# Twelve x tiles turned by VectorE from square blocks instead of by TensorE, in a fused attention and token-mixer kernel

## The chip, the cores and the metric

The kernel runs on one core of one Trainium2 chip. The metric is the device time of one execution in microseconds. A core has TensorE (PE, with its weight loads shown apart as PEld), VectorE (DVE), ScalarE (ACT), GpSimd (POOL) and SyncE (SP), which here issues nearly all DMAs. The engines run their own instruction streams and meet at semaphores.

## What is computed

x is 2048 tokens by 512 channels. Two branches read it, and a gate per token mixes them. All arrays are float32.

```python
def _A_ref(x, wqkv, wo):                       # B=1, S=2048, D=512, 32 heads of 16
    qkv = (x @ wqkv).reshape(B, S, 3, H, Dh).transpose(2, 0, 3, 1, 4)
    q, k, v = qkv[0], qkv[1], qkv[2]
    p = softmax(einsum("bhqd,bhkd->bhqk", q, k) * Dh ** -0.5, axis=-1)
    o = einsum("bhqk,bhkd->bhqd", p, v)
    return o.transpose(0, 2, 1, 3).reshape(B, S, D) @ wo

def _B_ref(x, w1, b1, w2, b2):                 # token mixer, F=1792
    h = layernorm(x, axis=-1)
    u = gelu(einsum("bsd,sf->bdf", h, w1) + b1)
    y = einsum("bdf,fs->bds", u, w2) + b2
    return y.transpose(0, 2, 1)

g = sigmoid((x * gate_w).sum(-1, keepdims=True))
return g * a + (1 - g) * b
```

## The kernel before

To keep float32 accuracy, every operand of a large matmul is split into a high part (a cast to float32r, by ACT) and a low part (the difference, by DVE or POOL); a product is three matmuls: high by high, high by low, low by high (`split` and `products`, L80 to L91).

The program runs through stages in this order, by the times of the profile: the V stage (to about 58 us), the projection of q and k (to 145 us), the mixer's first layer (to 297 us), and then attention with the mixer's second layer mixed in, until the end. PE works without a pause nearly all the way, so a stage begins when PE is done with the one ahead.

The V stage is what the change touches. It works on x in 16 tiles of 128 tokens. For each tile it does three things:

- The tile is turned, since a matmul contracts over partitions and x has its channels along the free axis. `turn(t)` has PE transpose the tile's four 128x128 chunks into a PSUM bank (L201); `turned(t)` casts the result into `xt_hi` (ACT) and subtracts into `xt_lo` (DVE, reading PSUM and SBUF). These two hold all of turned x, for V and later for q and k.
- V of the tile is computed: twelve matmuls (`products` with `v_pairs`, L90), then a copy out of PSUM by ACT (`v_out`, L235).
- `row_stats(t)` has DVE take the mean and the variance of each row (L212, L213) and the product with the gate's weights, summed (L215). These are needed later, for the layer norm and the gate.

The first two tiles are mixed with the arrival of the V weights in an order written out by hand (`tc.manual_schedule`, from L237). From tile 2 on a loop turns tile t + 1, takes the statistics of tile t - 2 and computes V of tile t; there the framework orders each engine's instructions by its own planner, except where `keep_in_program_order` holds them. SP loads each x tile with one DMA (`load`, L186) into one of six buffers. A DMA into a buffer waits until the last reader of the buffer is done, and whatever SP issues later stands behind it.

The weights of q and k come by `wcols` (L172), 128 columns at a time, in chunks k of 128 rows: chunk k of the turned x holds channels 128k to 128k + 127. Two of them are fetched and split within the loop, at t = 8 and t = 12. The biases of the mixer are loaded as rows, and PE turns them (L227) at t = 4.

Of the kernel before, what the change touches and what calls it, by code (L numbers as in the profile page):

```python
# [10 lines left out]
F32 = mybir.dt.float32  # L11
# [4 lines left out]
ALU = mybir.AluOpType  # L16
# [6 lines left out]
P = 128  # L23
S = 2048
D = 512
F = 1792
H = 32
DH = 16
NS = S // P
ND = D // P  # L30
NF = F // P
NB = 512
NQ = S // NB
VC = DH + 1
SCALE = DH**-0.5
# [40 lines left out]
def gated_mix(ctx: ExitStack, tc: tile.TileContext, a_x, a_wqkv, a_wo, b_w1, b_b1, b_w2, b_b2, gate_w, out):  # L76
    nc = tc.nc
    xf, of = (t.rearrange("b s d -> (b s) d") for t in (a_x, out))

    def split(hi, lo, src, copy, sub):  # L80

        copy(hi, src)  # L82
        return sub(lo, src, hi.bitcast(F32), ALU.subtract)  # L83

    def products(ps, pairs, start=True, stop=True):

        n, last = 0, 3 * len(pairs) - 1
        for (lh, ll), (rh, rl) in pairs:
            for a, b in ((lh, rh), (lh, rl), (ll, rh)):
                nc.tensor.matmul(ps, a, b, start=start and n == 0, stop=stop and n == last)  # L90
                n += 1  # L91
# [7 lines left out]
    ident = const.tile([P, P], F32, name="ident")  # L99
    make_identity(nc, ident)  # L100
    b1 = const.tile([P, NF], F32, name="b1")
    b2x2 = const.tile([P, NS], F32, name="b2x2")
    z = const.tile([P, NS], F32, name="z")
# [9 lines left out]
    v = v_pool.tile([P, NS, H, VC], F32, name="v")  # L113
# [5 lines left out]
    def bank():  # L119
        return acc.tile([P, NB], F32, name="acc")  # L120


    xt_pool = xt_ctx.enter_context(tc.tile_pool(name="xt", bufs=1, side="right"))
    xt_hi = xt_pool.tile([P, ND, S], F32R, name="xt_hi")
    xt_lo = xt_pool.tile([P, ND, S], F32R, name="xt_lo")
# [9 lines left out]
    loaded, ready, subs = [], [], []  # L135
# [27 lines left out]

    qk = qk_ctx.enter_context(tc.tile_pool(name="qk", bufs=2, side="right"))

    def wcols(c0):
        raw = qk.tile([P, ND, P], F32, name="wc_raw")
        hi = qk.tile([P, ND, P], F32R, name="wc_hi", bufs=3)
        lo = qk.tile([P, ND, P], F32R, name="wc_lo", bufs=3)
        src = a_wqkv[:, c0 : c0 + P].rearrange("(k p) c -> p k c", p=P)  # L170
        with tc.issue_after(x_load.ins):
            nc.sync.dma_start(raw, src)  # L172
        split(hi, lo, raw, nc.scalar.copy, nc.gpsimd.tensor_tensor)
        return hi, lo

    qk_cols = [c0 + b * P for b in range(ND) for c0 in (D, 0)]
    qk_w = []
    x_load = None

    with tc.tile_pool(name="vp", bufs=1, side="right") as pool:  # L180
        xs = {}

        def load(t):
            nonlocal x_load
            xs[t] = pool.tile([P, D], F32, name="x", bufs=6)
            x_load = nc.sync.dma_start(xs[t], xf[t * P : (t + 1) * P, :])  # L186

        gw = pool.tile([P, D], F32, name="gw")
        wv = []

        def load_wv(k):
            raw = pool.tile([P, D], F32, name=f"wv_raw{k}")
            nc.sync.dma_start(raw, a_wqkv[k * P : (k + 1) * P, 2 * D : 3 * D])  # L193
            wv.append((raw, pool.tile([P, D], F32R, name=f"wv_hi{k}"), pool.tile([P, D], F32R, name=f"wv_lo{k}")))

        turns = {}

        def turn(t, later=False):
            turns[t] = acc.tile([P, ND, P], F32, name="acc")
            for k in range(ND):  # L200
                nc.tensor.transpose(turns[t][:, k, :], xs[t][:, k * P : (k + 1) * P], ident)  # L201
            if not later:
                turned(t)

        def turned(t):
            cols = slice(t * P, (t + 1) * P)
            split(xt_hi[:, :, cols], xt_lo[:, :, cols], turns[t], nc.scalar.copy, nc.vector.tensor_tensor)

        def row_stats(t):

            st = pool.tile([P, 6], F32, name="stats", bufs=3)
            tc.keep_in_program_order(nc.vector.bn_stats(st, xs[t]))  # L212
            nc.vector.bn_aggr(mv[:, t, :], st)  # L213
            junk = pool.tile([P, D], F32, name="junk")
            dot = nc.vector.scalar_tensor_tensor(  # L215
                junk, xs[t], 1.0, gw, ALU.mult, ALU.mult, accum_out=z[:, t : t + 1]
            )
            tc.keep_in_program_order(dot)

        def biases(pool):  # L220
            for n, (src, dst, rows, mul) in enumerate(((b_b1, b1, NF, 1.0), (b_b2, b2x2, NS, 2.0))):

                t = pool.tile([P, P], F32, name=f"bias{n}")
                nc.gpsimd.memset(t, 0.0)
                nc.sync.dma_start(t[:rows], src.rearrange("(r c) -> r c", c=P))
                pt = bank()[:, :P]
                nc.tensor.transpose(pt, t, ident)  # L227
                nc.vector.tensor_scalar_mul(dst, pt[:, :rows], mul)

        def v_pairs(t):  # L230
            cols = slice(t * P, (t + 1) * P)
            return [((xt_hi[:, k, cols], xt_lo[:, k, cols]), wv[k][1:]) for k in range(ND)]

        def v_out(t, ps):
            nc.scalar.copy(v[:, t, :, 0:DH], ps.rearrange("p (h d) -> p h d", d=DH))  # L235

        with tc.manual_schedule():  # L237

            idle = pool.tile([P, NB], BF16, name="idle")
            nc.vector.memset(idle, 0.0)  # L240
            warm_ps = bank()

            def warm(n):
                for _ in range(n):
                    nc.tensor.matmul(warm_ps, idle[:, :P], idle, start=True, stop=True)

            warm(6)
            load(0)
            load_wv(0)
            load_wv(1)  # L250
            load(1)
            load_wv(2)
            load_wv(3)
            for t in (2, 3):
                load(t)
            nc.sync.dma_start(gw, gate_w[None, :].broadcast_to([P, D]))

            def split_wv(k):
                raw, hi, lo = wv[k]
                split(hi, lo, raw, nc.scalar.copy, nc.vector.tensor_tensor)  # L260


            two_ps = [bank(), bank()]

            def part(k, *which, last=False):

                for n, (t, a, b) in enumerate(which):
                    nc.tensor.matmul(  # L268
                        two_ps[t],
                        (xt_hi, xt_lo)[a][:, k, t * P : (t + 1) * P],  # L270
                        wv[k][1 + b],
                        start=k == 0 and a == b == 0,
                        stop=last and n >= len(which) - 2,
                    )

            split_wv(0)
            turn(0)
            warm(2)
            part(0, (0, 0, 0), (0, 0, 1), (0, 1, 0))
            split_wv(1)  # L280
            turn(1, later=True)
            part(1, (0, 0, 0), (0, 1, 0), (0, 0, 1))
            turned(1)
            part(0, (1, 0, 0), (1, 0, 1))
            part(1, (1, 0, 0), (1, 0, 1))
            part(0, (1, 1, 0))
            part(1, (1, 1, 0))
            both = [(t, *ab) for ab in ((0, 0), (1, 0), (0, 1)) for t in range(2)]
            split_wv(2)
            part(2, *both)  # L290
            split_wv(3)
            turn(2)
            part(3, *both, last=True)
            for t in range(2):
                v_out(t, two_ps[t])
        nc.gpsimd.memset(v[:, :, :, DH:VC], 1.0)
        load(4)
        load(5)
        for t in range(2, NS):
            if t + 4 < NS:  # L300
                load(t + 4)
            if t + 1 < NS:
                turn(t + 1)
            if t == 4:
                biases(pool)
            if t in (8, 12):
                qk_w.append(wcols(qk_cols.pop(0)))
            row_stats(t - 2)
            ps = bank()
            products(ps, v_pairs(t))  # L310
            v_out(t, ps)
        for t in range(NS - 2, NS):
            row_stats(t)
        pool.tile([P, 40], F32, name="pad")
        e = pool.tile([P, NS], F32, name="e")
        nc.scalar.activation(e, z, AF.Exp, scale=-1.0)
        nc.vector.tensor_scalar_add(e, e, 1.0)
        nc.vector.reciprocal(g, e)
        nc.vector.tensor_scalar(omg, g, -0.5, 0.5, ALU.mult, ALU.add)
        y, t, w = (pool.tile([P, NS], F32, name=n) for n in "ytw")  # L320
        nc.vector.tensor_scalar_add(w, mv[:, :, 1], EPS)
        nc.scalar.activation(y, w, AF.Sqrt)
        nc.vector.reciprocal(y, y)

        nc.vector.tensor_mul(t, y, y)
        nc.vector.tensor_mul(t, t, w)
        nc.vector.tensor_scalar(t, t, -0.5, 1.5, ALU.mult, ALU.add)
        nc.vector.tensor_mul(rs, y, t)
# [270 lines left out]
    rows = {}  # L599
# [581 lines left out]
```

## Time and profile before

| | |
|---|---|
| time, median of 3 runs | 1277.91 us |
| lowest and highest run | 1277.29, 1278.1 us |
| span of the profiled execution | 1276.0 us (its own time is not given apart; the span lies 1.9 us under the median) |
| PE busy | 1266.6 us (99%) |
| ACT, DVE, POOL busy | 1071.9 (84%), 719.3 (56%), 210.8 us (17%) |
| V stage's loop, tile 2's matmuls to the start of tile 14's | 13.66 to 52.33 us |

Rows of groups read: line, engine, operation, output<-inputs, shapes, count | busy us, mean ns of one | idle time of the engine before them and what ended it. Rows of the timeline read: start us, duration us, engine, line, operation, output<-inputs, and in brackets the idle time before. Rows of the chain read: start us, duration us, engine and line. Rows of windows give the busy time of each engine in a stretch, with the count of instructions, then the granted TensorE clock, the share of the 16 DMA engines in use, and GB/s. Rows of waits read: waiting engine and line, what it waited for, us in total, times, longest.

### The profile page before, as it was taken

The page shows a single profiled execution, that of the slowest core. Times are in us where ns is not written, and L with a number is a line of the kernel's source. Part 1 is how long each engine was busy: PE and PEld are TensorE (multiplying, and loading weights), DVE is VectorE, ACT ScalarE, POOL GpSimd, SP SyncE. Part 2 cuts the span into 40 slices and gives each one's busy share as a digit, 9 for nine tenths or more (in the row PEclk, how much of TensorE's full clock was granted, in tenths as well). Part 3 has the DMA queues.
Part 4 walks back from the last instruction along what each step waited for, and adds up shares of the span by engine and source line. Part 5 has one row for each costly group of instructions (what it writes and reads, how often), then busy time and mean ns, then how long its engine had stood idle before and what let it go on. Part 6 is the DMA issues. An engine that isn't in the chain of part 4 may idle for free.

```text
span 1276.0 us, 33051 instructions
## 1 busy us (share of the span) xinstructions
PE 1266.6 (99%) x13278; PEld 801.2 (63%) x13278; DVE 719.3 (56%) x1329; ACT 1071.9 (84%) x1484; POOL 210.8 (17%) x435
## 2 busy tenths in 40 slices
PE   9999999999999999999999999999999999999998
PEld 7888888886555555555555555555555555555555
DVE  5675363528776766666634346676666662325425
ACT  3444343437999999999999999999999999999994
POOL 0210144454111111111110011111111111100000
PEclk9999999999999999999999999999999999999999
DMA  4497743328443333433555533333343345446721
GB/s 133 141 304 274 241 122 99 99 71 166 84 93 59 74 76 70 79 70 76 116 107 115 129 77 69 69 72 76 68 78 72 74 82 109 98 88 198 149 62 70
DMA packets 94641, 137.37 MB, mean 108 GB/s; under 512 B 16313, under 2 KB 55375, under 8 KB 91408
## 3 DMA queue, kind: packets, MB, share of 16 engines
q1 hardware_dynamic: 93904, 134.14, 44.8%
q8 instruction: 106, 1.74, 0.6%
q10 hardware_dynamic: 576, 1.05, 0.2%
q14 instruction: 55, 0.45, 0.1%
HBM read 99.10 MB, written 36.03 MB: 106 GB/s over the span
## 4 chain that ended last, share of the span: by engine, by line
PE 99%; DMA 0%; ACT 0%; SPq 0%; DVE 0%; issue 0%
PE s L826 37%; PE s L868 34%; PE acc L429 12%; PE acc L90 10%; PE dn L989 4%; PE pa L1060 1%; PE acc L201 1%; PE dn L857 0%; PE acc L268 0%; DMA x<-in_A_x_dram 0%; ACT pt L891 0%; PE pa L1069 0%; SPq L193 0%; DVE base L1082 0%; SPq L186 0%
## 5 line engine op out<-in xcount | busy, mean ns | idle before, releaser
L891 ACT ACTIVATE pt<-s 128x512 f32<-128x512 f32 (+1 forms) x1259 | 943.5, 962 | 10.0 <-PE s L868 4.3
L868 PE MATMUL s<-qs,ks 64*128 64x512 f32 x2048 | 493.9, 404 | 0.8 <-POOL token L993 0.5
L826 PE MATMUL s<-pt,v 128*17 128x256 f32 x8024 | 482.6, 381 | 0.0
L868 PEld LDWEIGHTS s<-qs,ks 64*128 64x128 f32 x2048 | 325.4, 184 | 168.7 <-ACT pt L891 91.0
L846 DVE TENSOR_TENSOR ot<-s,ot 128x256 f32<-128x256 f32 (+2 forms) x427 | 190.4, 447 | 348.9 <-PE s L826 271.6
L826 PEld LDWEIGHTS s<-pt,v 128*17 128x17 f32 x8024 | 210.4, 97 | 232.2 <-ACT pt L891 84.2
L989 PE MATMUL dn<-u_hi,w_hi 64*128 64x512 f32 x428 | 186.4, 436 | 0.0
L83 POOL TENSOR_TENSOR w_lo<-w_raw,w_hi 128x512 fp32r<-128x512 f32 (+1 forms) x126 | 149.7, 1189 | 167.3 <-ACT w_hi L82 107.3
L989 PE MATMUL dn<-u_lo,w_hi 64*128 64x512 f32 x430 | 169.8, 395 | 0.0
L989 PE MATMUL dn<-u_hi,w_lo 64*128 64x512 f32 x430 | 169.2, 394 | 0.0
L993 POOL MEMSET token<- 1x1 f32 x256 | 26.2, 102 | 779.4 <-PE dn L989 711.8
L913 DVE SCALAR_TENSOR_TENSOR row<-row,o_hi 128x512 f32<-128x512 f32 x168 | 116.6, 694 | 4.9
L82 ACT CAST w_hi<-w_raw 128x512 fp32r<-128x512 f32 (+1 forms) x67 | 38.1, 569 | 79.4 <-PE acc L429 58.9
L429 PE MATMUL acc<-h_hi,w_hi 128*128 128x512 f32 x224 | 87.1, 389 | 0.0
L429 PE MATMUL acc<-h_lo,w_hi 128*128 128x512 f32 x224 | 87.1, 389 | 0.0
L429 PE MATMUL acc<-h_hi,w_lo 128*128 128x512 f32 x224 | 87.1, 389 | 0.0
L989 PEld LDWEIGHTS dn<-u_hi,w_lo 64*128 64x128 f32 x430 | 79.3, 184 | 1.3
L989 PEld LDWEIGHTS dn<-u_lo,w_hi 64*128 64x128 f32 x430 | 79.4, 185 | 0.4
L989 PEld LDWEIGHTS dn<-u_hi,w_hi 64*128 64x128 f32 x428 | 78.6, 184 | 1.1
L90 PE MATMUL acc<-xt_hi,wc_hi 128*128 128x512 f32 x128 | 49.8, 389 | 0.0
L90 PE MATMUL acc<-xt_lo,wc_hi 128*128 128x512 f32 x128 | 49.8, 389 | 0.0
L90 PE MATMUL acc<-xt_hi,wc_lo 128*128 128x512 f32 x128 | 49.8, 389 | 0.0
(145 smaller groups left out, 1148.5 us busy)
## 6 DMA issues: line engine op xcount, KB each, us to landing
w_raw<-in_B_w_dram SPq DMA_DIRECT2D x96, 256.0 KB
ks<-kp SPq DMA_DIRECT2D x192, 128.0 KB
qs<-qp SPq DMA_DIRECT2D x256, 64.0 KB
qp<-pc SPq DMA_DIRECT2D x16, 768.0 KB
x<-in_A_x_dram SPq DMA_DIRECT2D x32, 256.0 KB
kp<-pc SPq DMA_DIRECT2D x16, 512.0 KB
w_raw<-in_B_w_dram SPq DMA_DIRECT2D x32, 128.0 KB
bp<-row SPq DMA_DIRECT2D x16, 256.0 KB
```

The lines of the kernel that those rows point to most:

```text
L82: copy(hi, src)
L83: return sub(lo, src, hi.bitcast(F32), ALU.subtract)
L90: nc.tensor.matmul(ps, a, b, start=start and n == 0, stop=stop and n == last)
L201: nc.tensor.transpose(turns[t][:, k, :], xs[t][:, k * P : (k + 1) * P], ident)
L429: nc.tensor.matmul(p, a, b, start=first and k == 0, stop=last and k == 2)
L826: mm = nc.tensor.matmul(av[32 * j : 32 * j + VC, i * QC : (i + 1) * QC], v[:, c, g % NP * 2 + i, :], pt[:, h * QC : (h + 1) * QC], start=t ...
L846: reads(nc.vector.tensor_tensor(x, y, x, ALU.add), bank)
L868: mm = nc.tensor.matmul(banks[:, bank, :], kt[grp][rows, c * P : (c + 1) * P], qt[grp][rows, qb * NB : (qb + 1) * NB], start=True, stop=True,)
L891: act = nc.scalar.activation(dst, banks[:, at[0] : at[-1] + 1, :], AF.Exp, scale=SCALE)
L913: nc.vector.scalar_tensor_tensor(box[1], q or box[1], a, x, ALU.add, ALU.mult)
L989: mm = nc.tensor.matmul(ps, a[half], b[half], start=first and not second, stop=last and bool(second))
L993: fence = nc.gpsimd.memset(token, 0.0)
```

## The change

- Tiles 4 to 15 are no longer turned by PE. `load_blocks(t)` fetches the tile a second time, by four DMAs: block row q of the result holds, on partitions 32q to 32q + 31, channels 128q to 128q + 127 of the tokens, so that 32x32 blocks lie where a transpose within blocks needs them. `turn_blocks(t)` has DVE transpose all blocks in one instruction into `whole`, in SBUF; ACT casts it into `xt_hi`, and POOL subtracts into `xt_lo`. The x tile itself is still loaded, for `row_stats`.
- The channels are dealt to the four chunks in turn: chunk k holds channels k, k + 4, k + 8 and so on. The DVE transpose reads every fourth element for that, and so do the PE transposes of tiles 0 to 3; the loads of the weights of q, k and V deal their rows in the same way.
- The loop from tile 2 on is now within the order written out by hand. In turn t it does `turn_blocks(t + 2)`, `row_stats(t - 2)`, `load_blocks(t + 5)`, `load(t + 3)`, then V of tile t. The two loads of q/k weights are at t = 6 and 9, their splits at t = 9 and 12.
- The loads of the biases are issued in the first part, behind the blocks of tile 4; the first blocks are loaded there too.
- The warm-up matmuls go round three PSUM banks instead of one. x has five buffers instead of six; the blocks have four, the turned tiles two. The memset of V's column of ones comes inside the ordered part.

```diff
-        src = a_wqkv[:, c0 : c0 + P].rearrange("(k p) c -> p k c", p=P)
-        with tc.issue_after(x_load.ins):
-            nc.sync.dma_start(raw, src)
+        src = a_wqkv[:, c0 : c0 + P].rearrange("(p k) c -> p k c", k=ND)
+        nc.sync.dma_start(raw, src)
+        return raw, hi, lo
...
-            xs[t] = pool.tile([P, D], F32, name="x", bufs=6)
+            xs[t] = pool.tile([P, D], F32, name="x", bufs=5)
...
-            nc.sync.dma_start(raw, a_wqkv[k * P : (k + 1) * P, 2 * D : 3 * D])
+            nc.sync.dma_start(raw, a_wqkv.rearrange("(p k) c -> p k c", k=ND)[:, k, 2 * D : 3 * D])
...
-                nc.tensor.transpose(turns[t][:, k, :], xs[t][:, k * P : (k + 1) * P], ident)
+                nc.tensor.transpose(turns[t][:, k, :], xs[t].rearrange("p (r k) -> p k r", k=ND)[:, k, :], ident)
...
+        TURNED = 4
+        QUARTERS = P // BLOCK
+        blocks_of = {}
+
+        def load_blocks(t):
+            blocks_of[t] = pool.tile([P, QUARTERS, P], F32, name="xb", bufs=4)
+            src = xf[t * P : (t + 1) * P, :].rearrange("(a r) (q c) -> q r a c", r=BLOCK, q=QUARTERS)
+            for q in range(QUARTERS):
+                nc.sync.dma_start(blocks_of[t][q * BLOCK : (q + 1) * BLOCK], src[q])
+
+        def turn_blocks(t):
+            cols = slice(t * P, (t + 1) * P)
+            whole = pool.tile([P, ND, P], F32, name="xw", bufs=2)
+            nc.vector.transpose(
+                whole.rearrange("p k (a r) -> p k a r", r=BLOCK), blocks_of.pop(t).rearrange("p a (c k) -> p k a c", k=ND)
+            )
+            split(xt_hi[:, :, cols], xt_lo[:, :, cols], whole, nc.scalar.copy, nc.gpsimd.tensor_tensor)
...
-            warm_ps = bank()
+            warm_ps = [bank() for _ in range(3)]
...
             nc.sync.dma_start(gw, gate_w[None, :].broadcast_to([P, D]))
+            load_blocks(TURNED)
+            bias_tiles = load_biases(pool)
+            load_blocks(TURNED + 1)
+            load(4)
...
             part(3, *both, last=True)
+            load_blocks(TURNED + 2)
             for t in range(2):
                 v_out(t, two_ps[t])
-        nc.gpsimd.memset(v[:, :, :, DH:VC], 1.0)
-        load(4)
-        load(5)
-        for t in range(2, NS):
-            if t + 4 < NS:
-                load(t + 4)
-            if t + 1 < NS:
-                turn(t + 1)
-            if t == 4:
-                biases(pool)
-            if t in (8, 12):
-                qk_w.append(wcols(qk_cols.pop(0)))
-            row_stats(t - 2)
-            ps = bank()
-            products(ps, v_pairs(t))
-            v_out(t, ps)
-        for t in range(NS - 2, NS):
-            row_stats(t)
+            nc.gpsimd.memset(v[:, :, :, DH:VC], 1.0)
+            for t in range(2, NS):
+                if t + 1 < TURNED:
+                    turn(t + 1)
+                if t + 2 < NS:
+                    turn_blocks(t + 2)
+                row_stats(t - 2)
+                if t + 5 < NS:
+                    load_blocks(t + 5)
+                if t + 3 < NS:
+                    load(t + 3)
+                if t == 4:
+                    turn_biases(bias_tiles)
+                if t in (6, 9):
+                    qk_w.append(load_wcols(qk_cols.pop(0)))
+                if t in (9, 12):
+                    qk_w.append(split_wcols(*qk_w.pop(0)))
+                ps = bank()
+                products(ps, v_pairs(t))
+                v_out(t, ps)
+            for t in range(NS - 2, NS):
+                row_stats(t)
```

More of the change, by code (lines that the diff above doesn't have):

```diff
@@ L32 @@
 NB = 512
+BLOCK = 32
 NQ = S // NB
@@ L164, in gated_mix, with load_wcols @@
     qk = qk_ctx.enter_context(tc.tile_pool(name="qk", bufs=2, side="right"))
-    def wcols(c0):
+    def load_wcols(c0):
         raw = qk.tile([P, ND, P], F32, name="wc_raw")
@@ L169, in wcols, with split_wcols @@
         lo = qk.tile([P, ND, P], F32R, name="wc_lo", bufs=3)
-        src = a_wqkv[:, c0 : c0 + P].rearrange("(k p) c -> p k c", p=P)
-        with tc.issue_after(x_load.ins):
-            nc.sync.dma_start(raw, src)
+        src = a_wqkv[:, c0 : c0 + P].rearrange("(p k) c -> p k c", k=ND)
+        nc.sync.dma_start(raw, src)
+        return raw, hi, lo
+    def split_wcols(raw, hi, lo):
         split(hi, lo, raw, nc.scalar.copy, nc.gpsimd.tensor_tensor)
         return hi, lo
+    def wcols(c0):
+        with tc.issue_after(x_load.ins):
+            loaded = load_wcols(c0)
+        return split_wcols(*loaded)
     qk_cols = [c0 + b * P for b in range(ND) for c0 in (D, 0)]
@@ L207, in turned, with load_biases, turn_biases @@
             split(xt_hi[:, :, cols], xt_lo[:, :, cols], turns[t], nc.scalar.copy, nc.vector.tensor_tensor)
+        TURNED = 4
[13 more added lines that the diff above has]
+            split(xt_hi[:, :, cols], xt_lo[:, :, cols], whole, nc.scalar.copy, nc.gpsimd.tensor_tensor)
         def row_stats(t):
             st = pool.tile([P, 6], F32, name="stats", bufs=3)
-            tc.keep_in_program_order(nc.vector.bn_stats(st, xs[t]))
+            nc.vector.bn_stats(st, xs[t])
             nc.vector.bn_aggr(mv[:, t, :], st)
             junk = pool.tile([P, D], F32, name="junk")
[L215 to L223, printed above, removed]
+            nc.vector.scalar_tensor_tensor(junk, xs[t], 1.0, gw, ALU.mult, ALU.mult, accum_out=z[:, t : t + 1])
+        def load_biases(pool):
+            tiles = [pool.tile([P, P], F32, name=f"bias{n}") for n in range(2)]
+            for t, (src, rows) in zip(tiles, ((b_b1, NF), (b_b2, NS))):
                 nc.gpsimd.memset(t, 0.0)
                 nc.sync.dma_start(t[:rows], src.rearrange("(r c) -> r c", c=P))
+            return tiles
+        def turn_biases(tiles):
+            for t, (dst, rows, mul) in zip(tiles, ((b1, NF, 1.0), (b2x2, NS, 2.0))):
                 pt = bank()[:, :P]
@@ L240, in gated_mix @@
             nc.vector.memset(idle, 0.0)
-            warm_ps = bank()
+            warm_ps = [bank() for _ in range(3)]
             def warm(n):
-                for _ in range(n):
-                    nc.tensor.matmul(warm_ps, idle[:, :P], idle, start=True, stop=True)
+                for i in range(n):
+                    nc.tensor.matmul(warm_ps[i % 3], idle[:, :P], idle, start=True, stop=True)
             warm(6)
```

## The prediction

> **What bounds the kernel now.** I read the page's busy times first, then the chain of work in order of time, then the stage that the change touches by windows, groups and timeline.
>
> ```profile
> span 1276.0 us, 33051 instructions
> PE 1266.6 (99%) x13278; PEld 801.2 (63%) x13278; DVE 719.3 (56%) x1329; ACT 1071.9 (84%) x1484; POOL 210.8 (17%) x435
> 13.66 2.77 PE acc L90 x12
> 16.87 2.77 PE acc L90 x12
> 20.29 2.74 PE acc L90 x12
> ...
> 49.12 2.77 PE acc L90 x12
> 52.33 92.53 PE acc L90 x408
> core 0: us, PE busy (x) PEld busy (x) DVE busy (x) ACT busy (x) POOL busy (x), PEclk, DMA share, GB/s
> 13.40:52.30 38.90, 38.90 (x198) 32.16 (x197) 24.56 (x61) 14.98 (x29) 2.80 (x3) 1.00 0.39 113
> ```
>
> PE is busy for 99% of the span. In the V stage (13.4 to 52.3 us) it never stops, while DVE works 24.56 of 38.90 us, ACT 14.98, POOL 2.80, and the DMA engines 39%. So here each instruction taken from PE is worth its whole time, as long as the other engines keep up with the faster PE. The granted clock is 1.00 throughout.
>
> **What leaves PE.** The turns of tiles 4 to 15 lie in the twelve gaps between the group starts 13.66 and 52.33: 38.67 us. The block of 408 matmuls gives 92.53 / 408 = 0.227 us each, 2.72 for a tile's twelve, 32.66 for twelve tiles. The two bias transposes, which stay, are the difference between the second gap and the first: 3.42 - 3.21 = 0.21. So the 48 transposes cost 38.67 - 32.66 - 0.21 = **5.8 us**, all of it on the path.
>
> **What takes their place.** Per turned tile: one DVE transpose, an ACT cast that now reads SBUF, a subtraction that moves from DVE to POOL, four block DMAs.
>
> ```profile
> L83 DVE TENSOR_TENSOR xt_lo<-acc,xt_hi 128x512 fp32r<-128x512 f32 x16 | 11.1, 691 | 18.4 <-ACT xt_hi L82 18.4
> L83 DVE TENSOR_TENSOR wv_lo<-wv_raw,wv_hi 128x512 fp32r<-128x512 f32 x4 | 2.7, 689 | 4.6 <-ACT wv_hi L82 4.6
> L1032 DVE TENSOR_TENSOR sums<-ot,sums 128x256 f32<-128x256 f32 x2 | 0.8, 424 | 0.1
> L1029 DVE STREAM_TRANSPOSE turned<-ot 128x256 f32<-128x256 f32 x2 | 0.9, 445 | 0.1
> L413 DVE TENSOR_REDUCE far<-most_row 1x32 f32<-1x512 f32 x1 | 1.0, 1045 | 0.0
> L372 DVE TENSOR_REDUCE kmax<-acc 128x1 f32<-128x512 f32 x16 | 10.9, 681 | 0.2 <-DVE rs L328 0.2
> L83 POOL TENSOR_TENSOR wc_lo<-wc_raw,wc_hi 128x512 fp32r<-128x512 f32 x8 | 11.2, 1401 | 96.2 <-ACT wc_hi L82 95.4 <-DMA w_raw<-in_B_w_dram 0.8
> L201 PEld LDWEIGHTS acc<-ident,x 128*128 128x128 f32 x64 | 7.9, 141 | 3.1 <-DMA x<-in_A_x_dram 0.7 <-issue 0.5
> ```
>
> The transpose is bounded thus. A transpose of 256 contiguous elements takes 0.445 us; 512 add what they add to a two-input operation (0.689 - 0.424 = 0.265): 0.71. But the new one reads every fourth element. The nearest row with such a step is the L413 reduce, whose inner step is four floats: 1.045 against 0.681 for a contiguous 512, so 0.36 more, though it also writes 32 results. That gives 1.07. I take 1.05, with 0.71 and 1.24 (0.445 + three times 0.265, every element costing double) as ends. The Trainium skill ("SBUF — State Buffer", the cacheline note under Door 1) says that SBUF has 16-byte lines and that each access to a new line pays a penalty, so four fp32 is as far as one strides for free; it speaks for the upper half, and the L413 row agrees. A penalty of a full access per element would make 1.24, which leaves the sum below as it is.
>
> The same step is in the weight loads of the four tiles still turned on PE: 16 loads at 0.141 us. They cost between nothing and a doubling (2.2 us); by the ratio of the two reduces (1.53) it is 1.2, and since a load runs beside the matmul before it I take half, **0.6 us**. Nothing in a longer step can make a load faster, so there is no gain here.
>
> DVE then needs, for a tile, the transpose and the row statistics:
>
> ```profile
> 50.43 0.69 DVE L83 TENSOR_TENSOR xt_lo<-acc,xt_hi 128x512 fp32r<-128x512 f32 x1 [1.72 <-ACT xt_hi L82]
> 51.04 0.68 DVE L212 BATCH_NORM_STATS2 stats<-x 128x6 f32<-128x512 f32 x1
> 51.86 0.66 DVE L215 SCALAR_TENSOR_TENSOR junk<-x,gw 128x512 f32<-128x512 f32 x1
> 52.44 0.08 DVE L215 DVE_READ_ACCUMULATOR junk<-x,gw 128x1 f32 x1
> 52.10 1.57 POOL L83 TENSOR_TENSOR wc_lo<-wc_raw,wc_hi 128x512 fp32r<-128x512 f32 x1 [0.81 <-DMA w_raw<-in_B_w_dram]
> 49.30 0.62 ACT L82 CAST wc_hi<-wc_raw 128x512 fp32r<-128x512 f32 x1
> 49.99 1.30 POOL L83 TENSOR_TENSOR wc_lo<-wc_raw,wc_hi 128x512 fp32r<-128x512 f32 x1 [8.40 <-ACT wc_hi L82]
> 61.17 0.08 DVE L215 DVE_READ_ACCUMULATOR junk<-x,gw 128x1 f32 x1
> 61.29 0.22 ACT L316 ACTIVATE e<-z 128x16 f32<-128x16 f32 x1 [2.85 <-DVE junk L215]
> ```
>
> The statistics run 1.40 us (51.04 to 52.44), and an instruction starts 0.08 before the one ahead of it ends (50.43 + 0.69 against 51.04). So a tile costs DVE 1.05 - 0.08 + 1.40 = 2.37 of PE's 2.72, and up to a transpose of 1.40 us DVE holds the pace. ACT has 0.62 + 0.59 = 1.2, POOL 1.30: both fit.
>
> **Queues.** SP issues five DMAs for a tile instead of one.
>
> ```profile
> 4.52 0.43 SPq L256 DMA_DIRECT2D gw<-in_gate_w_dram  x1
> SPq L186 <- DVE junk L215: 33.4, 10, 8.7
> 36.00:39.50 3.50, 3.50 (x20) 2.93 (x19) 2.06 (x5) 1.37 (x3) 0.00 (x0) 1.00 0.56 150
> 44.00:45.50 1.50, 1.50 (x9) 1.19 (x8) 1.47 (x5) 0.00 (x0) 0.00 (x0) 1.00 0.52 168
> ```
>
> At 0.43 each that is 2.15 us of 2.72. SP still blocks on `load(t + 3)` until DVE has read tile t - 2 (the 33.4 us of waits now); behind that wait stand the next tile's blocks, which DVE wants only three tiles later, 8 us. One x load holds all DMA engines for 0.52 x 1.5 = 0.78 us; the 36.0 to 39.5 window holds one x load and one wc load (512-byte rows, like the blocks) in 0.56 x 3.5 = 1.96, so 1.18 for the latter. Together 1.96 of 2.72 us: it fits, and I charge nothing; were the blocks twice as dear, 3.14 us would bound the stage. The bias loads pass behind tile 4's blocks instead of behind x; their transposes come at tile 4, some 10 us later. The wc loads and their splits move, and the q/k stage wants them only after tile 15. The V-weight rows keep their 2 KB runs. The extra warm-up banks and the memset of v lie ahead of PE's first work or beside it. All this: 0.
>
> **Sum.** Span 1276.0 - 5.8 + 0.6 = 1270.8. The page gives no other time for its execution; its span stands 1.9 under the median of 1277.91, so **1272.7 us**. After the stage nothing is late: the row statistics, which now trail behind tile 15, are done before it, and PE's work to the end only slides forward.
>
> **Rival 1, a serial loop through the port of DVE and POOL: slower.** POOL's subtraction and DVE's gate product (L215) read two SBUF tensors each, and the trace shows that such a pair takes turns.
>
> ```profile
> 14.62 0.69 DVE L83 TENSOR_TENSOR xt_lo<-acc,xt_hi 128x512 fp32r<-128x512 f32 x1 [1.44 <-ACT xt_hi L82]
> 178.05 1.30 POOL L83 TENSOR_TENSOR w_lo<-w_raw,w_hi 128x512 fp32r<-128x512 f32 x1 [1.42 <-ACT w_hi L82]
> 178.52 1.37 DVE L83 TENSOR_TENSOR h_lo<-hf,h_hi 128x512 fp32r<-128x512 f32 x1 [0.89 <-ACT h_hi L82]
> L83 DVE TENSOR_TENSOR h_lo<-hf,h_hi 128x512 fp32r<-128x512 f32 x8 | 5.4, 679 | 0.0
> 180.77 1.29 POOL L83 TENSOR_TENSOR w_lo<-w_raw,w_hi 128x512 fp32r<-128x512 f32 x1 [1.42 <-ACT w_hi L82]
> 180.89 1.19 DVE L414 TENSOR_SCALAR far<-far 1x32 f32<-1x32 f32 x1
> 281.13 0.69 DVE L443 TENSOR_TENSOR gs<-gs,gu 128x512 f32<-128x512 f32 x1
> 281.19 1.23 POOL L83 TENSOR_TENSOR w_lo<-w_raw,w_hi 128x256 fp32r<-128x256 f32 x1 [0.38 <-ACT w_hi L82]
> ```
>
> The h_lo subtraction took 1.37 instead of 0.68 and ended half a microsecond after POOL's; the POOL operation at 52.10 took 1.57 instead of 1.30 because L215 was there first. Today's subtraction reads PSUM and passes freely (50.43, beside POOL's 49.99, took 0.69). The Trainium skill ("SBUF — State Buffer", Two separate sides) calls this an exclusive lock, held for the whole instruction by whoever starts first; these rows agree.
>
> Who starts first after a DVE transpose? POOL: 0.04 to ACT (61.25 to 61.29), 0.62 cast, 0.07 to POOL (49.92 to 49.99): 0.73 after its end. L215: 0.82 after the statistics begin (51.04 to 51.86), which begin 0.08 before it: 0.74. A tie. A DVE start 0.06 ahead of POOL's won (281.13), one 0.12 behind lost (180.89). If L215 wins, DVE turns a tile every 2.37 us and runs ahead until ACT's casts wait behind PE; later collisions are then hidden by that lead. If POOL wins each time, L215 waits out the subtraction and the next transpose waits for L215: 1.05 + 0.73 + 1.16 + 0.58 = 3.52 us a tile, over 2.72 and over today's 3.22 (1.16 is POOL's 1.30 less the 0.14 by which h_lo's 178.52 + 1.37 - 0.68 falls ahead of POOL's end; 0.58 is from L215's start to the next instruction's, 51.86 to 52.44). DVE is free for tile 4's transpose at 15.2 (14.62 + 0.69 - 0.08), so the tile is ready at 15.2 + 1.05 + 0.73 + 1.30 = 18.3, tile 15 eleven rounds of 3.52 later at 57.0, its matmuls done at 59.7 where today's end at 52.33 + 2 x 2.72 = 57.8: +1.9 + 0.6, **1280.4 us**. With a transpose of 0.71 it is 3.18 a round and 1276.4; with 1.24, 3.71 and 1282.7. It decides for slower than before above a transpose of about 0.85 us.
>
> **Rival 2, DVE itself too slow.** A transpose over 1.40 us: each 0.1 beyond costs about 1.2 us less the two tiles of lead; at 1.8 the stage would end near 57, no gain, 1277.7. Nothing in the rows goes so far.
>
> **Rival 3, the gain is given back** by DMAs that arrive late or by the next stage: about 1277.5. Against it: PE was never starved in the 92.53 us that follow, and DMA demand before them has room.
>
> **How the numbers follow.** Forecast 0.57; rival 1 0.31 (a tie, leaning to L215 since the known losing distance is double the winning one; slower 0.16, no change 0.11, faster 0.04, by the transpose's length); rival 2 0.05 (slower 0.03, no change 0.02); rival 3 0.07 (slower 0.03, no change 0.04). About 0.2% (2.6 us) is what a measurement here can tell from none. Faster 0.61, same 0.17, slower 0.22. The forecast's own range is 1271.5 (no dearer weight loads, and the 0.6 by which the lowest run lies under the median) to 1274.3 (weight loads doubled); the range for all cases reaches up past rival 1's middle: 1271.5 to 1281.0.
>
> **What would show it.** Right: between tiles 4 and 15 PE groups start every 2.72 us, no L201 after tile 3, the q/k block starts near 47, DVE's transpose about 1.05, L215 sometimes 1.2 and more but no PE wait. Wrong: PE waiting on POOL's xt_lo with rounds of 3.2 to 3.7 us, each L215 near 1.8 (rival 1); a transpose over 1.4 (rival 2); PE or DVE waiting on the block DMA, or pauses after the q/k block starts (rival 3).

## The result, and the profile after

The changed kernel takes 1272.41 us (median; 1271.8 to 1272.6), before 1277.91: a ratio of 0.9957 with a 95% interval of 0.9945 to 0.9969, so 5.5 us faster. 1272.7 was forecast.

The page of the changed kernel, its chain of work in order of time, and its V stage by windows (columns as before):

```profile
span 1270.4 us, 33041 instructions
PE 1261.4 (99%) x13230; PEld 797.6 (63%) x13230; DVE 725.9 (57%) x1329; ACT 1072.8 (84%) x1484; POOL 229.4 (18%) x447
13.33 5.48 PE acc L91 x24
19.03 119.71 PE acc L91 x528
138.74 149.39 PE acc L464 x660
288.56 6.21 DMA ks<-kp
294.79 3.24 DMA qs<-qp
298.03 0.47 PE s L903
13.40:46.60 33.20, 33.20 (x149) 27.44 (x148) 31.79 (x66) 15.31 (x28) 22.49 (x14) 1.00 0.72 202
```

PE still has no pause in the V stage, with 33.20 of 33.20 us, but DVE now has 31.79 where it had 24.56 of 38.90, and the DMA engines are used at 72% instead of 39%. The chain is one block of 528 matmuls where it had a group for each tile. Two more rows of the kernel before, from its chain, give the later edges:

```profile
144.85 152.32 PE acc L429 x672
303.52 0.44 PE s L868
```

Four stretches account for the difference of the spans, 1276.0 - 1270.4 = 5.6 us:

| stretch | before | after | difference |
|---|---|---|---|
| to the loop's first matmuls | 13.66 | 13.33 | -0.33 |
| from there to the first layer (144.85, 138.74) | 131.19 | 125.41 | -5.78 |
| from there to attention's first scores (303.52, 298.03) | 158.67 | 159.29 | +0.62 |
| from there to the end | 972.48 | 972.37 | -0.11 |

The second row is the change. The first and the third are dealt with below.

The groups of the V stage and one round of its timeline, in the changed kernel:

```profile
L230 DVE STREAM_TRANSPOSE xw<-xb 128x512 f32<-128x512 f32 x12 | 13.2, 1096 | 0.1
L84 POOL TENSOR_TENSOR xt_lo<-xw,xt_hi 128x512 fp32r<-128x512 f32 x12 | 20.0, 1667 | 21.3 <-ACT xt_hi L83 21.3
L209 PEld LDWEIGHTS acc<-ident,x 128*128 128x128 f32 x16 | 2.7, 209 | 0.7 <-issue 0.5
17.24 1.10 DVE L230 STREAM_TRANSPOSE xw<-xb 128x512 f32<-128x512 f32 x1
18.26 0.66 DVE L238 BATCH_NORM_STATS2 stats<-x 128x6 f32<-128x512 f32 x1
18.37 0.62 ACT L83 CAST xt_hi<-xw 128x512 fp32r<-128x512 f32 x1 [1.28 <-DVE xw L230]
19.05 0.66 DVE L241 SCALAR_TENSOR_TENSOR junk<-x,gw 128x512 f32<-128x512 f32 x1
19.07 1.79 POOL L84 TENSOR_TENSOR xt_lo<-xw,xt_hi 128x512 fp32r<-128x512 f32 x1 [0.60 <-ACT xt_hi L83]
19.64 1.09 DVE L230 STREAM_TRANSPOSE xw<-xb 128x512 f32<-128x512 f32 x1
35.33 1.29 POOL L84 TENSOR_TENSOR wc_lo<-wc_raw,wc_hi 128x512 fp32r<-128x512 f32 x1
35.95 1.22 DVE L241 SCALAR_TENSOR_TENSOR junk<-x,gw 128x512 f32<-128x512 f32 x1
```

The gate product (now L241) starts at 19.05 and POOL's subtraction at 19.07. POOL lost that race by 0.02 us and paid for it: 1.79 us instead of 1.30. DVE did not wait, so its round is 17.24 to 19.64, 2.40 us. So it goes in the first seven of the twelve rounds, each time by 0.02 to 0.03 us. From the eighth on ACT's cast stands behind its copy of V, which waits for PE (DVE has run ahead, as the prediction said it would), and the order changes from round to round: at 35.95 a subtraction of q/k weights is on POOL first, and the product takes 1.22 us. PE waits for none of it. The near-tie that the prediction worked out is there to within 0.03 us, and it came out the faster way.

### The profile page after: what moved, and what is told of

It is laid out like the page before. It is cut to its first block, busy times and chain, and to the rows that moved or that the text cites. A ratio compares the mean times of both kernels' runs of the same rounds, so it can differ in the third digit from the quotient of the medians.

```text
span 1270.4 us, 33041 instructions
## 1 busy us (share of the span) xinstructions
PE 1261.4 (99%) x13230; PEld 797.6 (63%) x13230; DVE 725.9 (57%) x1329; ACT 1072.8 (84%) x1484; POOL 229.4 (18%) x447
## 3 DMA queue, kind: packets, MB, share of 16 engines
q10 hardware_dynamic: 576, 1.05, 0.2%
## 4 chain that ended last, share of the span: by engine, by line
PE 98%; DMA 1%; ACT 0%; DVE 0%; issue 0%; SPq 0%
PE s L861 38%; PE s L903 33%; PE acc L464 12%; PE acc L91 10%; PE dn L1024 4%; PE pa L1095 1%; PE acc L298 0%; DMA ks<-kp 0%; ACT pt L926 0%; PE acc L271 0%; DMA qs<-qp 0%; PE pa L1104 0%; PE acc L209 0%; DVE base L1117 0%; SPq L149 0%
```

## Experiments

Theory A is the prediction's: each turn that leaves PE is worth 0.48 us, provided that the gate product reaches the shared port ahead of POOL's subtraction. Its rivals: the two tiles of lead hide that order anyway (B); the gain has other sources in the change, the order by hand or the moved loads (C).

**late_dot: push the gate product behind POOL.**

```diff
             nc.vector.bn_aggr(mv[:, t, :], st)
+            nc.vector.tensor_scalar_mul(pool.tile([P, 1], F32, name="spare", bufs=3), mv[:, t, 0:1], 1.0)
             junk = pool.tile([P, D], F32, name="junk")
```

> The changed kernel with one tiny DVE operation (128x1, about 0.1 us) between the statistics and the gate product, so that the product starts some 0.1 us later. Theory A (who takes the shared port first decides; in the changed kernel the gate product wins by 0.02 to 0.03 us): POOL now wins every time, each round is 1.10 + 0.74 + 1.16 + 0.58 = 3.58 us, tile 15's matmuls end near 60.1 instead of 51.7, and the kernel takes 1280.8 us, slower than before the change. Rival theory B (PE's two tiles of lead hide who goes first): 1272.4 to 1273.0.

Measured 1281.11 us, ratio to before 1.0024 [1.0014, 1.0033]. A round of its timeline, the group of its products, and the largest wait of PE's weight loads:

```profile
17.61 1.30 POOL L84 TENSOR_TENSOR xt_lo<-xw,xt_hi 128x512 fp32r<-128x512 f32 x1 [15.11 <-ACT xt_hi L83]
17.70 0.15 DVE L240 TENSOR_SCALAR spare<-mv 128x1 f32<-128x1 f32 x1
17.77 1.69 DVE L242 SCALAR_TENSOR_TENSOR junk<-x,gw 128x512 f32<-128x512 f32 x1
19.39 1.09 DVE L230 STREAM_TRANSPOSE xw<-xb 128x512 f32<-128x512 f32 x1
L242 DVE SCALAR_TENSOR_TENSOR junk<-x,gw 128x512 f32<-128x512 f32 x15 | 22.1, 1475 | 0.0
PEld acc L91 <- POOL xt_lo L84: 8.9, 10, 1.1
```

The product starts 0.16 us behind POOL and takes 1.69 us; the next transpose waits for it, and a round takes 3.6 us (15.78 to 19.39 and 19.39 to 22.98). PE's weight loads now wait for POOL. One DVE operation on 128x1 elements, 0.15 us by its record, turned a gain of 5.5 us into a loss of 3.2. B falls, provided that it is not the operation as such that costs the time, which the next run tells.

**tail_op and tail_even: the same operation behind the product.**

```diff
             nc.vector.scalar_tensor_tensor(junk, xs[t], ...)
+            nc.vector.tensor_scalar_mul(pool.tile([P, 1], F32, name="spare", bufs=3), mv[:, t, 0:1], 1.0)
```

> The changed kernel with the same tiny DVE operation placed behind the gate product. Control for late_dot: DVE does the same work, the order at the port stays. Both theories: DVE's round grows from 2.39 to about 2.5 us, under PE's 2.72, so 1272.4 us. If it is as slow as late_dot, it is DVE's load and not the order at the port.

Measured 1273.5 us, ratio 0.9965 [0.9953, 0.9978]. So it is the order and not the load: the same operation and the same tile, only behind the product, cost 7.6 us less. But 1.1 us more than the changed kernel's stayed unexplained: PE waited for nobody, yet the chain's block of the V stage was longer.

```profile
20.16 120.78 PE acc L91 x528
```

Against 119.71 for the same 528. Its V matmuls start every 0.234 us instead of 0.227, at a granted clock of 1.00; those of q and k do not. In late_dot, which has the same spare tile, the V matmuls that do not wait start every 0.234 us too. The spare tile lies in the pool of the V weights, so it may have moved their addresses. tail_even widens the tile (`pool.tile([P, 64], F32, name="spare", bufs=2)[:, :1]`).

> tail_op with its spare tile widened to 256 bytes a partition, two of them, so that the tiles behind it keep the addresses modulo 512 that they have in the changed kernel. In tail_op the V stage's matmuls started every 0.234 us instead of 0.227, which is its 1.1 us. Theory E (the moving operand's address costs it): 0.227 and 1272.4 us. Rival (the extra DVE operation itself slows the loop): 0.234 and 1273.5 again.

Measured 1272.39 us, ratio 0.9958 [0.9944, 0.9971], and the block is back:

```profile
19.80 119.71 PE acc L91 x528
```

Only the size and the number of the spare tiles changed (three of 4 bytes a partition, then two of 256), and the 1.1 us went; the operation itself costs nothing here. That the moving operand's address is what does it is the reading that fits, but it is not shown: no trace gives the addresses. The gain of the change is not of this kind: in the kernel before, the matmuls behind the last turn start every 0.227 us as well (92.53 us for 408).

**turned10 and turned16: give turns back to PE.**

```diff
-        TURNED = 4
+        TURNED = 10        # and 16
```

with guards so that no blocks are loaded or turned for the tiles left to PE.

> The changed kernel, but only tiles 10 to 15 are turned by DVE; tiles 4 to 9 are turned by PE again (24 transposes back on PE), no blocks loaded for them. Theory A (the gain is the transposes' time on PE, 0.48 us a tile): 1272.4 + 6 x 0.48 = 1275.3 us. Rival C (the gain comes from the order written out by hand, the moved loads or the start): under 1273.4.

> The changed kernel with all 16 tiles turned by PE: everything else of the change (dealt columns, order by hand, moved loads) without its main part. Theory A: 1272.4 + 12 x 0.48 = 1278.2 us, or 1277.6 if what is lost again at attention's start (0.6 us) is not lost here. Rival C: under 1275. Rival D (the weight loads with a step of four floats, 0.209 us instead of 0.141, cost PE in a full loop): 48 x 0.07 = 3.3 us more, 1281.5.

Measured 1275.82 us, ratio 0.9985 [0.9976, 0.9994], and 1280.66, ratio 1.0023 [1.0013, 1.0033]. Their chains, turned10's first:

```profile
13.37 2.76 PE acc L91 x12
23.45 2.77 PE acc L91 x12
26.70 2.77 PE acc L91 x12
142.03 149.39 PE acc L466 x660
14.14 2.76 PE acc L91 x12
53.88 92.52 PE acc L91 x408
146.40 149.39 PE acc L466 x660
```

From the loop's start to the first layer the changed kernel takes 125.41 us, turned10 128.66 and turned16 132.26: 0.54 us for each of six turns, 0.57 for each of twelve. So the gain goes with the number of turns, and C falls: all of the change without its main part is slower than before. The 0.06 to 0.09 above 0.48 is partly the dealt columns' price on PE (next). turned16 is 8.3 us slower than the changed kernel, 1.4 more than its loop explains: 0.8 is its later start (14.14), and what is lost at attention's start was lost there as well and more, against what I expected. Its 1280.66 lies nearer to rival D's 1281.5 than to 1278.2; whether the weight loads are the reason is the question of the next run.

**dealt_before and no_step: the price of reading every fourth element.** dealt_before is the kernel before with the dealt columns alone. no_step is the changed kernel with neighbouring channels read instead, while the weights stay dealt; it leaves out the match of channels and weights, and serves for its time alone:

```diff
-  xs[t].rearrange("p (r k) -> p k r", k=ND)[:, k, :]        # PE
+  xs[t][:, k * P : (k + 1) * P]
-  blocks_of.pop(t).rearrange("p a (c k) -> p k a c", k=ND)  # DVE
+  blocks_of.pop(t).rearrange("p a (k c) -> p k a c", k=ND)
```

> The kernel before the change with the dealt columns alone: all 16 tiles turned by PE with a step of four floats, weights of q, k and V dealt to match. Theory A (0.09 us a turn in the full loop, 14 turns): 1277.9 + 1.3 = 1279.2 us. Rival (the weight loads hide beside the matmuls): 1277.9. By the 0.6 us that the prediction charged for four tiles it would be 1277.9 + 2.4 = 1280.3.

> The changed kernel with the DVE transposes and the PE turns of tiles 0 to 3 reading channels that lie side by side instead of every fourth one; the weights stay dealt, so the channels meet the wrong weights. Theory A (the step costs DVE 0.4 us a tile, but DVE is not on the path; it costs PE 0.09 us a turn, as in turned16): transposes of 0.71 instead of 1.10 us, weight loads of 0.141 instead of 0.209, 1272.4 - 4 x 0.09 = 1272.0 us. Rival (DVE's round bounds the loop): 12 x 0.39 = 4.7 us less, 1267.7.

Measured 1278.97 us, ratio 1.0009 [1.0, 1.0018], and 1272.07, ratio 0.9952 [0.9938, 0.9965]. Two groups of dealt_before's chain and its weight loads, then two groups of no_step:

```profile
27.19 2.77 PE acc L90 x12
30.44 2.77 PE acc L90 x12
L201 PEld LDWEIGHTS acc<-ident,x 128*128 128x128 f32 x64 | 10.3, 205 | 2.4 <-DMA x<-in_A_x_dram 0.8 <-issue 0.6
L230 DVE STREAM_TRANSPOSE xw<-xb 128x512 f32<-128x512 f32 x12 | 8.5, 706 | 2.0 <-DMA xb<-in_A_x_dram 2.0
L209 PEld LDWEIGHTS acc<-ident,x 128*128 128x128 f32 x16 | 2.2, 160 | 1.8 <-DMA x<-in_A_x_dram 1.0 <-issue 0.6
```

The step costs a DVE transpose 1.096 - 0.706 = 0.39 us, and yet to take it away leaves the time where it was: DVE is not on the path. On PE, the 64 weight loads go from 0.141 to 0.205 us from the kernel before to dealt_before (the 16 of the first tiles from 0.160 in no_step, where I expected 0.141, to 0.209 in the changed kernel), but the pitch of the tiles only from 3.21 to 3.25: 0.04 us for a turn. My 0.09 for dealt_before was too much, and rival D falls: the rest of what turned16 lost to turns is not the step's. In turned16's chain four turns take 0.57 to 0.72 us where all of dealt_before's in the loop take 0.47; that is about 0.6 us, and what held them stays open. dealt_before's 1.2 us, hardly clear of none, are 0.5 in the loop (131.68 to the first layer against 131.19) and otherwise its start and attention.

**turn_twice: DVE beyond PE's pace.**

```diff
-            nc.vector.transpose(whole..., blocks...)
+            for _ in range(2):
+                nc.vector.transpose(whole..., blocks...)
```

> The changed kernel with every DVE transpose done twice into the same tile. DVE's round becomes 2.39 + 1.02 = 3.41 us, beyond PE's 2.72, the order at the port stays. Prediction's threshold (DVE holds the pace up to a transpose of 1.40 us; beyond it the excess less the lead is paid): 11 x 0.69 = 7.6, about 1280 us. Rival (DVE has more room than that, waits being hidden by the buffers): under 1275.

Measured 1281.67 us, ratio 1.0029 [1.0018, 1.004]. Two starts of its timeline, each of both transposes of a tile, and the wait of PE's weight loads:

```profile
18.99 2.22 DVE L232 STREAM_TRANSPOSE xw<-xb 128x512 f32<-128x512 f32 x2
22.51 2.22 DVE L232 STREAM_TRANSPOSE xw<-xb 128x512 f32<-128x512 f32 x2
PEld acc L91 <- POOL xt_lo L84: 10.5, 12, 1.1
```

The round is 3.52 us, 0.8 over PE's pace, and 9.3 us are lost. So DVE has no hidden room: what it has in a round is 2.72 less 2.40, 0.3 us.

**dot_first: the gate product ahead of the statistics**, so 0.8 us ahead of POOL (`row_stats` has L241 before L238).

> The changed kernel with the gate product put ahead of the statistics in row_stats, so that it is at the shared port 0.8 us before POOL instead of 0.03. Theory A: POOL's subtraction falls from 1.67 to 1.30 us, DVE's round stays 2.39, PE's pace stays 2.72: 1272.4 us, and no cliff nearby. Rival: the order by chance cost something in each round even now (POOL waits 0.5 us for the product): up to 1 us faster.

Measured 1272.31 us, ratio 0.9954 [0.9941, 0.9968]; POOL's subtraction:

```profile
L84 POOL TENSOR_TENSOR xt_lo<-xw,xt_hi 128x512 fp32r<-128x512 f32 x12 | 16.4, 1366 | 26.4 <-ACT xt_hi L83 26.4
```

The same time as the changed kernel, without its edge: POOL takes 1.37 instead of 1.67, and nothing gains by it, since POOL too was beside the path. DVE's round became 2.5 us (18.20 to 20.73), not the 2.39 expected, and is still under PE's 2.72.

**after_again and dot_first_again: how far the start and attention's first rows wander.**

> The changed kernel once more, unaltered. The loop of the V stage began at 13.33 us in its profile, at 13.66 before the change, at 14.33 and 14.14 in tail_op and turned16, with the landing of tile 1's x. If that is a property of the program: 1272.4 us again and a start at 13.3. If it belongs to the placement or the single execution: up to 1273.4 and a start up to 14.3, and 0.3 to 1 us in every comparison here are not the change's.

> dot_first once more, unaltered, for its profile. The turn of tile 1 began at 7.40 us there and at 6.65 in both profiles of the changed kernel, though nothing that runs before that moment differs. If the landing of x belongs to the program, it begins at 7.4 again; if it belongs to the execution, anywhere from 6.6 to 7.6. In both cases 1272.3 us, since what is gained there is lost again where attention's first q rows land.

Measured 1272.43, ratio 0.9956 [0.9943, 0.997], and 1272.09, ratio 0.9953 [0.9933, 0.9973]. PE took up tile 1 at 6.66 and 6.65 us in the two profiles of the changed kernel, at 7.39 and 6.80 in the two of dot_first, which is one and the same kernel: it belongs to the execution. The profile of dot_first that started its loop late, at 14.18, had no wait for q rows later:

```profile
14.18 5.48 PE acc L91 x24
139.59 152.32 PE acc L464 x672
291.91 6.35 PE dn L892 x28
298.25 0.42 PE s L903
```

From 139.59 to 298.25 it takes 158.66 us, as before the change; the changed kernel, 0.85 ahead at 138.74, takes 159.29, because its chain there runs through the DMAs of ks and qs. Of the 0.85 only 0.22 is left. But that loss belongs to the execution as well: after_again, the same kernel, takes 158.77 us for the stretch (138.85 to 297.62), and dot_first_again, as early in its loop (13.47), takes 158.6 (138.88 to 297.48) and keeps its lead, with a span of 1270.0 us against dot_first's 1270.6. That an early start is lost again at this place, as I expected, is seen in one profile of three.

**turned2: tiles 2 and 3 turned by DVE too**, their blocks loaded ahead of their x.

> The changed kernel with tiles 2 and 3 turned by DVE too: their blocks are loaded in place of their x, which comes later, for the statistics. Theory A (0.48 us for each turn that leaves PE): 1272.4 - 0.96 = 1271.4 us. Rival (in the first 13 us DMA, ACT and POOL are late for tile 2, so PE waits): 1272.4 or more.

Measured 1273.19 us, ratio 0.9962 [0.9949, 0.9976]: no better than the change. Its chain at the start, and the waits of PE's weight loads and of PE:

```profile
4.99 5.50 DMA xb<-in_A_x_dram
10.93 1.09 DVE xw L230
12.04 0.63 ACT xt_hi L83
12.74 1.29 POOL xt_lo L84
14.07 5.29 PE acc L91 x22
PEld acc L91 <- POOL xt_lo L84: 1.1, 1, 1.1
PE acc L91 <- POOL xt_lo L84: 0.6, 1, 0.6
```

PE starts on tile 2 at 12.7, with the two matmuls that need only `xt_hi`, and then stands still for 0.6 us, since the way over block, transpose, cast and subtraction ends at 14.03. The rival was right: the path over DMA, DVE, ACT and POOL needs a lead that the first tiles do not have. No version tried beats the changed kernel by more than its interval.

## Why the prediction was right

- **What leaves PE** was right: 5.8 us from the gaps between groups, 5.78 measured from the loop's start to the first layer. turned10 and turned16 show the same price, and a little more, from the other side.
- **The DVE transpose** was sized at 1.05 and measured 1.10; from the round worked out as 2.37, 2.40 came. The row it was sized by, a reduce with a step of four floats, served well: 0.36 more there, 0.39 here. The Trainium skill's note on 16-byte lines ("SBUF — State Buffer", Door 1) agrees in direction. The price is 0.39 us for 512 elements, 0.76 ns each; an element without the step costs 1.02 ns, by the 0.706 us for 512 here and the 0.445 for 256 before. So it is about three quarters of an element's time, not a whole one.
- **The weight loads of the turns on PE** were the term that was mis-sized: 0.6 us for four tiles. The loads did become 45% longer (0.141 to 0.205), but the loop's pitch shows 0.04 us a turn, which makes 0.16 for four. That only half of a longer load would be hidden was a guess; nearly all of it is. The start that was to be 0.6 later was 0.33 earlier, and that belongs to the execution: over the profiles of the kernels that turn tiles 0 to 3 on PE it lies between 13.33 and 14.33.
- **"After the stage nothing is late"** was wrong by 0.6 us in the profiled execution: at attention's start the DMAs of ks and qs were late. In after_again it was 0.1, with 0.3 more in the rest, at the same span. It nearly offsets the term above, so that the total came within 0.3 us, closer than its parts, is luck.
- **Queues**: five DMAs a tile at 1.96 of 2.72 us were predicted, 72%; the window shows a DMA share of 0.72. It holds loads of the later stages' weights too, so the agreement to the hundredth is chance; that the queues keep pace is not.
- **Rival 1** did not happen, but by 0.02 us. The prediction had POOL ahead by 0.01 (0.73 against 0.74 after the transpose's end). POOL came after 0.73, but the product after 0.71, since it starts 0.79 us after the statistics and not 0.82. So that DVE went first was luck as far as the prediction goes: the forecast leaned to it by two distances, 0.06 and 0.12, that say nothing of 0.02. late_dot is that rival: 3.6 us a round where 3.52 was worked out, 1281.1 us where 1280.4 was.
- **Rival 2** was not met, with a transpose of 1.10. turn_twice goes 0.8 beyond the 1.40 that was given as the threshold and pays for it; where exactly the threshold lies was not tested.
- **The signs** that it named came: no turn by PE after tile 3, matmuls every 0.227 us without a wait (2.72 a tile), a product of 1.2 us now and then without cost to PE. Tile 14's matmuls, which it put near 47, start at 46.1 us, by the start and the mis-sized term above.

## What to carry to other kernels

Where PE is busy without a pause, each instruction moved off it is worth its whole pitch, read from the gaps between groups and not from its own duration. What takes its place is harmless as long as its round, waits at shared ports included, is shorter than PE's, and its first results are ready when PE comes to them; so work out who comes first at such a port, and if it is a tie, reorder the engine's own instructions until it is none. An experiment that adds a tile can change the time by its size alone, apparently because the other tiles move: give it a size that leaves them in place, and see whether the time changes.

## What was not expected of the hardware

- Two starts 0.02 us apart decide the order at the port that DVE and POOL share: with L241 ahead by 0.02 to 0.03, in seven rounds on end, POOL's 1.30 us became 1.79 each time, and with L242 0.16 behind, DVE's 0.66 became 1.69.
- Three spare tiles of 4 bytes a partition in the pool of the V weights lengthened the V matmuls' start interval from 0.227 to 0.234 us (3%) in the mean, at an unchanged granted clock, in tail_op and late_dot alike; two of 256 bytes did not.
- Weight loads of PE whose elements lie 16 bytes apart take 0.205 instead of 0.141 us, and next to nothing of it reaches the matmuls behind them: 0.04 us for the four loads of a turn.
